# Five of the 36 input loads issued as two transfers, of 100 and of 28 partitions

## The chip, the cores and the metric

The kernel runs on one core of a Trainium2 chip. The metric is the device time of one execution in microseconds; the time of a kernel is the median of its runs. A separate execution of each kernel was recorded by the hardware profiler, and everything called "the profile" or "the trace" below comes from that one execution. The engines are named as the profile names them: PE (TensorE matmul), PEld (TensorE weight load), DVE (VectorE), ACT (ScalarE), POOL (GpSimd) and SP (SyncE, which here does nothing but issue DMAs). "SPq" is SP's instruction queue. The DMA transfers run on 16 DMA engines.

## The reference

Two stages are computed in one kernel. The first is a retention recurrence over 768 steps for 4 batches and 8 heads of 64 dimensions, the second a token mixer whose weights come from its own input:

```python
def _attn_ref(q, k, v):                       # q, k, v: (4, 8, 768, 64) float32
    gamma = 1.0 - 2.0 ** (-5.0 - np.arange(H, dtype=np.float32))
    scale = 1.0 / np.sqrt(D)
    for t in range(S):
        state = gamma[None, :, None, None] * state + np.einsum('bhd,bhe->bhde', k[:, :, t], v[:, :, t])
        y[:, :, t] = scale * np.einsum('bhd,bhde->bhe', q[:, :, t], state)
    return y

def _moe_ref(x, w_q, w_k, w_out):             # x: y as (4, 768, 512)
    wq, wk = x @ w_q, x @ w_k
    W_tok = scale * np.einsum('bsd,btd->bst', wq, wk)
    mixed = np.einsum('bst,btd->bsd', W_tok, x)
    return np.maximum(mixed, 0.0) @ w_out
```

The output is (4, 768, 512) in float32.

## The kernel before

**Tiling.** The 768 steps of a batch are three *pairs* of two 128-token chunks; four batches make the pairs 0 to 11. For each pair three loads bring q, k and v: 256 tokens of all 8 heads, 512 KB each. Partition g of a load holds the tokens 2g and 2g+1 of the pair, so each of the 128 partitions gets, for each of the 8 heads, one contiguous run of 2 x 64 floats, 512 bytes. That makes 128 x 8 = 1,024 runs of 512 bytes in a load.

**Loads.** `LOADS` (line 53) is the order of the loads, written out by hand: `... q3 w v3 k4 q4 k5 v4 q5 o1 o0 v5 k6 q6 v6 q7 k7 v7 k8 q8 v8 q9 k9 k10 v9 q10 k11 v10 q11 v11`, then the stores `s0 s5 ...`. `w` is the two small projection weights, `o0` and `o1` are four transfers of `w_out`. All of them are issued by SP, in this order (one half of k0 alone is issued by ACT). `load_pair` (line 157) issues the transfer of a pair: one `dma_start` over 128 partitions. The staging tiles `q_st`, `k_st`, `v_st` are 7 slots of three pairs each; a slot is loaded anew once the three pairs in it have been cast.

**Casts.** Before TensorE can use a load, another engine casts it to bf16: `cq`, `ck` and `cv` (`cv` also multiplies by a power of the decay, `fv`). `ORDER` (line 16) is one list of all steps, written out by hand; the letter behind a step is the engine that takes it (A for ACT, V for DVE, P for POOL). Every engine executes its own steps strictly in this order, so a step that waits holds back all later steps of its engine. `ck.5.0:P` is the cast of the first chunk of k of pair 5, on POOL. For the pairs from 2 on a `ck` or a `cv` of one chunk is two instructions of 64 partitions; the copies stand in the profile under the helper's lines 133 (ACT) and 134 (POOL, DVE), the `cv` under line 619.

**The steps that read the five loads of the change**, with their engines:

| load | steps | what stands behind them on the engine |
|---|---|---|
| v3 | `cv.3.0:P`, `cv.3.1:P` | `cq.4:P`, `ck.5.0:P`, `cv.4.0:P` |
| v4 | `cv.4.0:P`, `cv.4.1:P` | `WO.1:P` (a cast of `w_out`), `cv.5.0:P`, `cv.5.1:P`, `cq.6:P` |
| k7 | `ck.7.0:P`, `ck.7.1:P` | `ck.8.0:P`, `ck.8.1:P` |
| q9 | `cq.9:A` | `es.7.1:A`, `ck.9.1:A` |
| q10 | `cq.10:P` | `cv.9.1:P`, `cv.10.0:P` |

**The rest of a pair.** TensorE transposes k and q (`trk`, `trq`, lines 648 to 685), forms the scores `sc` (707), the running state `st` (758), the parts of y (`in` 744, `ia` 778), transposes x (`xt` 811, 818), projects it (`wqk` 841, 850), accumulates `zm` over a batch (875), and for each pair computes `mx` (894) and the output projection `pj` (916). DVE and ACT evict what TensorE leaves in PSUM. The last steps are `pj` and the evictions `eo`, after which SP issues the last stores (line 945).

Of the kernel before, what the change touches and what calls it, by code (L numbers as in the profile page):

```python
# [59 lines left out]
OBUFS = 9  # L60
CASTS = dict(k=6, v=6, q=4)
WBYTES = 1024
OBYTES = 2048
KQS = 2

# [2 lines left out]
def kernel(  # L68
# [15 lines left out]
    nc = tc.nc  # L84
# [4 lines left out]
    C = 128  # L89
    G = C // 2  # L90
    NP = S // (2 * C)
    NG = B * NP
    NDM = DM // 128
    HP = H // 2
# [48 lines left out]
    def slot(key):  # L143
        if key not in slots:
            slots[key] = stage_pool.tile([128, 3 * 2 * H * D], FP32, name=key + "_st", tag="st")
        return slots[key]
# [8 lines left out]
    SOURCES = {"k": k, "q": q, "v": v}  # L155

    def load_pair(name, p, half=None, eng=None):
        st = pairs[p]
        st[name + "_st"] = slot(name + str(p // NP)).rearrange(
            "p (cp x hp j d) -> p cp x hp j d", cp=NP, x=2, hp=HP, j=2  # L160
        )[:, p % NP]
        xs = slice(0, 2) if half is None else slice(half, half + 1)
        (eng or nc.sync).dma_start(
            out=st[name + "_st"][:, xs].rearrange("g x hp j d -> g (x hp) (j d)"),
            in_=SOURCES[name][
                p // NP, xs.start * HP : xs.stop * HP, p % NP * 2 * C : (p % NP + 1) * 2 * C, :
            ].rearrange(
                "h (g j) d -> g h (j d)", j=2
            ),
        )  # L170

    def load_batch(name, b):
        st = slot(name + str(b))
# [19 lines left out]
    def load_weights(token):  # L193
# [5 lines left out]
        else:  # L199
# [3 lines left out]
            for i in range(2):  # L203
                a = 2 * n + i
                nc.sync.dma_start(
                    out=st[:, i], in_=moe_w_out[128 * a : 128 * a + 128, :], max_dma_last_dim=WBYTES
                )
        wstages[token] = st

    def load_token(token):  # L210
        if token[0] in "wo":
            load_weights(token)
        elif token[0] in "KQV":
            load_batch(token[0].lower(), int(token[1:]))
        else:
            load_pair(token[0], int(token[1:]))
# [3 lines left out]
    freed = {}  # L220

    load_pair("k", 0, 0, nc.scalar)
    load_pair("k", 0, 1, nc.sync)

    def more_loads():
        while queue:
            token = queue[0]
            if token[0] == "s":
                if not stored(token[1:]):
                    return  # L230
                queue.pop(0)
                continue
            key = slot_of(token)
            if key not in staged:
                n = len(staged)
                if n >= SLOTS and freed.get(staged[n - SLOTS], 0) < 3:
                    return
                staged.append(key)
            load_token(queue.pop(0))
# [64 lines left out]
    for cp in range(NP):  # L304
        nc.gpsimd.tensor_copy(
            out=fy1.rearrange("p (cp x) c hp -> p cp x c hp", x=2)[:, cp].rearrange("p x c hp -> p c x hp"),
            in_=fy[:, 2 * cp : 2 * cp + 2].rearrange("p c (hp x) -> p c x hp", x=2),
# [627 lines left out]
    def stored(name):  # L935
        p, _, j = name.partition("/")
        p, js = int(p), [int(j)] if j else [0, 1]
        if not all((p, i) in evicted for i in js):
            return False
        b, cp = divmod(p, NP)  # L940
        dst = out[b, cp * 2 * C : (cp + 1) * 2 * C, :].rearrange("(g j) m -> g j m", j=2)
        src = pairs[p]["o"]
        if j:
            dst, src = dst[:, int(j)], src[:, int(j)]
        nc.sync.dma_start(out=dst, in_=src, max_dma_last_dim=OBYTES)
        return True

    steps2 = dict(
# [6 lines left out]
        st=state1, es=es1, ia=ia1, **{"in": inter1}, ex=ex1,  # L955
# [48 lines left out]
```

## Time and profile before

| what | us |
|---|---|
| median of 3 runs | 98.84 (98.34 to 99.11) |
| the profiled execution, its own time | 97.45 |
| its span, first to last instruction | 95.7 |
| PE busy | 83.9 (88% of the span) |
| DVE busy | 73.4 (77%) |
| ACT busy | 67.3 (70%) |
| POOL busy | 65.2 (68%) |

The profiled execution took 97.45 us by the same clock as the runs, 1.75 us more than its span, and 1.39 us less than their median. The granted TensorE clock was 0.997 over the span. The page that the profiler leaves has busy times, a strip of 40 slices, the DMA queues, a chain of waits that is followed back from the last instruction, and the costliest groups of instructions. Here the strip shows POOL busy until slice 32 and then idle, and PE busy from slice 2 to the end. From HBM 20.19 MB were read and 6.29 MB written.

In the lines of the profile `v_st<-in_v_dram` is a load of v, `vs<-v_st,fv` its cast, and a bracket behind a timeline line is the idle time ahead of it with what ended it. A busy share over the whole span mixes stages with different limits; the waits of a stage tell more.

### The profile page before, as it was taken

To read this page: it belongs to the slowest core of one execution; us is meant where nothing else is said; L and a number is where in the kernel's file an instruction comes from. 1 tells how busy PE (TensorE), PEld (TensorE's weight loads), DVE (VectorE), ACT (ScalarE), POOL (GpSimd) and SP (SyncE) were. 2 spreads that over 40 slices of the span, in tenths; PEclk is the share of its full clock that TensorE was granted. 3 is DMA by queue.
4 is the path that set the end of the run, shared out by engine and by line. 5 is a ranking of instruction groups with operands and counts; after the bars stand their busy time and mean duration, and the time that the engine had idled before them with its cause. 6 is when DMAs were issued, how large, how long until landed. Compare 5 with 4: busy or idle time off the path is not lost.

```text
span 95.7 us, 3878 instructions
## 1 busy us (share of the span) xinstructions
PE 83.9 (88%) x1677; PEld 53.6 (56%) x1695; DVE 73.4 (77%) x105; ACT 67.3 (70%) x102; POOL 65.2 (68%) x85
## 2 busy tenths in 40 slices
PE   4999799695788989999998999999999999999920
PEld 1334565574666657546786558677675775644400
DVE  3243986979799996995999999998999966547400
ACT  4200439968775689799997999999999755455640
POOL 4696870798899795999999999899999920000000
PEclk9999999999999999999999999999999999999998
DMA  1999999999999999999999999999679000919992
GB/s 32 283 347 347 346 345 310 288 260 265 280 327 299 344 332 334 311 334 339 298 297 337 323 332 303 265 302 326 217 280 374 28 0 39 394 71 403 399 377 80
DMA packets 42929, 26.73 MB, mean 279 GB/s; under 512 B 1952, under 2 KB 39840, under 8 KB 42912
## 3 DMA queue, kind: packets, MB, share of 16 engines
q1 hardware_dynamic: 42384, 26.22, 87.9%
q10 hardware_dynamic: 528, 0.26, 0.9%
q8 instruction: 13, 0.21, 0.8%
q14 instruction: 4, 0.03, 0.1%
HBM read 20.19 MB, written 6.29 MB: 277 GB/s over the span
## 4 chain that ended last, share of the span: by engine, by line
PE 62%; DVE 10%; ACT 8%; POOL 8%; issue 7%; DVEq 0%; ACTq 0%
PE banks L916 17%; PE banks L381 10%; POOL ks L134 5%; DVE at_sb L719 4%; PE banks L778 4%; PE banks L894 3%; PE banks L707 3%; ACT ks L133 3%; POOL vs L619 3%; PE banks L850 3%; PE banks L818 3%; PE banks L758 3%; PE banks L841 2%; PE banks L875 2%; PE banks L648 2%
## 5 line engine op out<-in xcount | busy, mean ns | idle before, releaser
L619 POOL TENSOR_TENSOR vs<-v_st,fv 64x512 bf16<-64x512 f32 x36 | 37.6, 1043 | 4.5 <-DMA v_st<-in_v_dram 2.5
L719 DVE TENSOR_TENSOR at_sb<-banks,cmaskr 128x1024 bf16<-128x1024 f32 x20 | 23.8, 1215 | 0.7 <-PE banks L707 0.6
L916 PE MATMUL banks<-wout_sb,relu 128*128 128x512 bf16 x82 | 22.2, 380 | 1.1 <-issue 0.5
L133 ACT CAST ks<-k_st 64x512 bf16<-64x512 f32 (+1 forms) x25 | 15.8, 634 | 9.3 <-DMA k_st<-in_k_dram 8.8
L133 ACT COPY o_st<-banks 128x512 f32<-128x512 f32 x19 | 11.2, 588 | 3.6 <-PE banks L916 3.6
L792 DVE TENSOR_TENSOR x_nat<-banks,fy 128x1024 bf16<-128x1024 f32 x10 | 12.2, 1222 | 1.8 <-PE banks L744 1.5
L916 PEld LDWEIGHTS <-relu 128*128 128x128 bf16 x96 | 8.2, 98 | 9.0 <-issue 1.2
L909 ACT ACTIVATE relu<-banks 128x1024 bf16<-128x1024 f32 x11 | 11.3, 1024 | 1.6 <-PE banks L916 1.0
L381 PE MATMUL banks<-warm 128*128 128x512 bf16 x31 | 10.6, 479 | 1.8 <-DVE warm L255 1.3
L134 POOL CAST ks<-k_st 64x512 bf16<-64x512 f32 x16 | 11.1, 695 | 1.1 <-DMA k_st<-in_k_dram 0.2
L134 DVE COPY kq<-banks 128x1024 bf16<-128x1024 bf16 x14 | 9.4, 687 | 3.2 <-PE banks L431 1.9
L133 ACT COPY kq<-banks 128x1024 bf16<-128x1024 bf16 x10 | 10.0, 1012 | 2.5 <-PE banks L431 1.7
L134 POOL CAST qs<-q_st 128x1024 bf16<-128x1024 f32 (+1 forms) x7 | 6.9, 986 | 3.1 <-DMA q_st<-in_q_dram 2.7
L707 PE MATMUL banks<-kq 64*128 64x128 bf16 x160 | 7.5, 217 | 0.3 <-DVE xT L134 0.3
L778 PE MATMUL banks<-vs,at_sb 128*128 128x64 bf16 x160 | 7.3, 193 | 0.2 <-DVE at_sb L719 0.2
L850 PE MATMUL banks<-xT,wqk_w 128*128 128x256 bf16 x48 | 7.2, 273 | 0.0
L381 PEld LDWEIGHTS <-warm 128*128 128x128 bf16 x35 | 3.4, 115 | 5.8 <-issue 3.4
L778 PEld LDWEIGHTS <-at_sb 128*128 128x128 bf16 x160 | 5.9, 98 | 1.1 <-DVE at_sb L719 0.3
L707 PEld LDWEIGHTS <-kq 64*128 64x128 bf16 x160 | 4.8, 94 | 3.0 <-issue 2.8
L133 ACT COPY xT<-banks 128x1024 bf16<-128x1024 bf16 x5 | 5.1, 1013 | 1.7 <-PE banks L818 1.6
L134 DVE COPY xT<-banks 128x1024 bf16<-128x1024 bf16 x7 | 4.8, 688 | 1.7 <-PE banks L818 0.8
L133 ACT CAST qs<-q_st 128x1024 bf16<-128x1024 f32 x5 | 5.2, 1049 | 1.1 <-DMA q_st<-in_q_dram 1.0
(83 smaller groups left out, 130.4 us busy)
## 6 DMA issues: line engine op xcount, KB each, us to landing
q_st<-in_q_dram SPq DMA_DIRECT2D x12, 512.0 KB, 6.6
v_st<-in_v_dram SPq DMA_DIRECT2D x12, 512.0 KB, 6.3
k_st<-in_k_dram SPq DMA_DIRECT2D x11, 512.0 KB, 7.1
out_dram<-o_st SPq DMA_DIRECT2D x9, 512.0 KB, 3.6
out_dram<-o_st SPq DMA_DIRECT2D x6, 256.0 KB, 2.3
w_st<-in_moe_w_out_dram SPq DMA_DIRECT2D x4, 256.0 KB, 5.2
k_st<-in_k_dram ACTq DMA_DIRECT2D x1, 256.0 KB, 3.8
k_st<-in_k_dram SPq DMA_DIRECT2D x1, 256.0 KB, 3.5
```

What stands on the lines that cost most here:

```text
L133: return nc.scalar.copy(out=out, in_=in_)
L134: return ENGINES[e].tensor_copy(out=out, in_=in_)
L381: nc.tensor.matmul(out=bank32(b), lhsT=warm[:, 0:128], rhs=warm, start=True, stop=True)
L619: ENGINES[e].tensor_tensor(out=tokens_st(p, "v")[rows(j), c].rearrange("p hp x d -> p (hp x) d"), in0=pair_st(p, "v")[rows(c), :, j], in1= ...
L707: nc.tensor.matmul(out=ps[:, x, hi, c, :], lhsT=st["kT"][rows(x), hp, c, :], rhs=st["qT"][rows(x), hp, c, :], start=(hi == 0 and c == 0), ...
L719: ENGINES[e].tensor_tensor(out=st["at", half].rearrange("p x hi c t -> p (x hi c) t"), in0=st["at_ps", half].rearrange("p (n t) -> p n t", ...
L758: nc.tensor.matmul(out=state_ps[rows(x), hp, :], lhsT=st["ks"][:, c, hp, x, :], rhs=st["vs"][:, c, hp, x, :], start=(cp == 0 and c == 0 an ...
L778: nc.tensor.matmul(out=y[:, x, c, hp, :], lhsT=st["at", half][:, x, hi, c, :], rhs=st["vs"][:, c, hp, x, :], start=first1(p, x), stop=Fals ...
L792: nc.vector.tensor_tensor(out=st["x"].rearrange("p c a i n -> p (c a i n)").rearrange("p (m x d) -> p x m d", x=2, d=D), in0=st["y_ps"].re ...
L850: nc.tensor.matmul(out=st["w_ps"][:, 128:384], lhsT=wqk_sb[:, a, DH:], rhs=st["xT"][:, a].rearrange("p c t -> p (c t)"), start=False, stop ...
L909: nc.scalar.activation(out=dst, in_=st["mx_ps"], func=ACT.Relu)
L916: nc.tensor.matmul(out=bank32(b), lhsT=st["relu"][:, a, j, :], rhs=wout_sb[:, a, :], start=(a == 0), stop=(a == NDM - 1),)
```

## The change

`load_pair` looks up the load's name in a table of cut points. Five loads are in it, each cut at partition 100; each of these is issued as two `dma_start`s one after the other on the same queue, partitions 0 to 99 and 100 to 127. All other loads have one piece, as before. The stores get the same loop with an empty table, so they stay one transfer.

```diff
 WBYTES = 1024
+PARTS = {'v3': (100,), 'v4': (100,), 'k7': (100,), 'q9': (100,), 'q10': (100,)}
+SPLIT = {}
 OBYTES = 2048
...
-        (eng or nc.sync).dma_start(
-            out=st[name + "_st"][:, xs].rearrange("g x hp j d -> g (x hp) (j d)"),
-            in_=SOURCES[name][
-                p // NP, xs.start * HP : xs.stop * HP, p % NP * 2 * C : (p % NP + 1) * 2 * C, :
-            ].rearrange(
-                "h (g j) d -> g h (j d)", j=2
-            ),
-        )
+        dst = st[name + "_st"][:, xs].rearrange("g x hp j d -> g (x hp) (j d)")
+        src = SOURCES[name][
+            p // NP, xs.start * HP : xs.stop * HP, p % NP * 2 * C : (p % NP + 1) * 2 * C, :
+        ].rearrange("h (g j) d -> g h (j d)", j=2)
+        cuts = [0, *PARTS.get(name + str(p), ()), C]
+        for lo, hi in zip(cuts, cuts[1:]):
+            (eng or nc.sync).dma_start(out=dst[lo:hi], in_=src[lo:hi])
...
-        nc.sync.dma_start(out=dst, in_=src, max_dma_last_dim=OBYTES)
+        cuts = [0, *SPLIT.get(name, ()), G * 2]
+        for lo, hi in zip(cuts, cuts[1:]):
+            nc.sync.dma_start(out=dst[lo:hi], in_=src[lo:hi], max_dma_last_dim=OBYTES)
```

## The prediction

> **What bounds the kernel now.** I read the page first, then the instruction queue of SP in order of time, then the idle gaps of POOL, then the chain of waits where POOL hands over to PE.
>
> ```profile
> PE 83.9 (88%) x1677; PEld 53.6 (56%) x1695; DVE 73.4 (77%) x105; ACT 67.3 (70%) x102; POOL 65.2 (68%) x85
> ...
> DMA  1999999999999999999999999999679000919992
> ...
> q8 instruction: 13, 0.21, 0.8%
> ```
>
> PE is the busiest engine. The DMA engines are busy without a break until slice 28 (67 us), so the loads are a stream that can set the pace too. The third line is traffic that the kernel did not issue: 13 packets of 16 KB that carry instructions. They use the same DMA engines.
>
> SP's queue, in order of time (start, duration):
>
> ```profile
> 1.28 0.50 SPq L163 DMA_DIRECT2D q_st<-in_q_dram  x1
> 1.82 0.57 SPq L163 DMA_DIRECT2D v_st<-in_v_dram  x1
> ...
> 10.67 1.40 SPq L163 DMA_DIRECT2D v_st<-in_v_dram  x1
> 12.12 3.02 SPq L163 DMA_DIRECT2D k_st<-in_k_dram  x1
> ...
> 22.68 2.43 SPq L163 DMA_DIRECT2D k_st<-in_k_dram  x1
> ...
> 42.60 2.52 SPq L163 DMA_DIRECT2D k_st<-in_k_dram  x1
> ...
> 55.85 2.82 SPq L163 DMA_DIRECT2D k_st<-in_k_dram  x1
> ```
>
> An issue that nothing holds up takes 0.5 us. Later ones take 1.4, which is the pace at which the DMA engines drain: SP waits for room. Four take 2.4 to 3.0. Instruction packets of 0.95 us start at 13.29, 23.67, 42.26 and 56.21 us, inside three of these four issues and 0.34 ahead of the other. (The rest of the packets go with shorter stops, such as 1.80 at 48.12; the longest issue of all, 3.32 at 33.24, follows four short ones for `w_out` that had filled the queue.) So one held-up DMA engine stops SP, and with it the supply of all sixteen.
>
> The trace also has sixteen landing marks for each transfer, one per DMA engine. Before 13 us a transfer's marks lie within 0.45 us and each comes exactly 1.512 us after the same mark of the transfer ahead: every engine moves 64 runs and one closing mark, 65 packets of 23.3 ns, eight rows each. It is a limit of each engine by packets, not of a shared pipe: the 256 KB transfers of `w_out`, with runs of 1 KB, land 0.68 us apart (385 GB/s against 347). For q2, behind the packet of 13.29, fifteen marks lie at 14.76 to 15.24 as expected and the sixteenth at 16.46. The others are unmoved, so the packet hit one engine, the one that had been twelfth to land.
>
> Where the loads reach the computation, POOL's timeline:
>
> ```profile
> 24.29 4.37 POOL L619 TENSOR_TENSOR vs<-v_st,fv 64x512 bf16<-64x512 f32 x4 [0.54 <-DMA v_st<-in_v_dram]
> ...
> 31.69 4.36 POOL L619 TENSOR_TENSOR vs<-v_st,fv 64x512 bf16<-64x512 f32 x4 [0.51 <-DMA v_st<-in_v_dram]
> ...
> 38.10 4.38 POOL L619 TENSOR_TENSOR vs<-v_st,fv 64x512 bf16<-64x512 f32 x4 [0.94 <-DMA v_st<-in_v_dram]
> ```
>
> These are the casts of v3, v4 and v5; the brackets are idle time ended by their loads. After 38.10 POOL has no gap until 77, so when v5 lands sets POOL's schedule from there on. It reaches PE twice:
>
> ```profile
> 50.33 0.97 POOL ks L134
> 51.30 0.05 issue
> 51.35 0.37 PE banks L648 x13
> ...
> 63.97 1.05 POOL vs L619
> 65.02 0.04 issue
> 65.06 0.32 PE banks L758 x8
> ```
>
> PE's matmuls start 0.32 us late at 51.35 and 0.39 late at 65.06 (spacing of starts, less the usual spacing of the line). Elsewhere from 36 to 92 us PE hardly pauses. So a gain in loads is worth at most about 0.7 us, while a loss at v5 goes through whole.
>
> **The change part by part.** *Shares.* A 128-row load gives each engine 8 rows. No transfer of another height is in the trace. If the shares stay equal, as all marks show for 128, 100 rows go to ten engines with 10 each (10 is the largest divisor of 100 up to 16) and 28 rows to fourteen with 2 each. If both start from the same first engine, ten engines get 12 rows (96 runs, 2 marks: 98 x 23.3 ns = 2.28 us, +0.77), four get 2 rows (0.40 us, -1.12) and two get none (-1.51). The other bound is an even spread, 0. I take the first, since every transfer of the trace is shared equally. The Trainium skill, "DMA: Bandwidth & Descriptors", section "Why a DMA increments its semaphore by 16 and not by 1", states this rule, with the lowest-numbered engines used; no run before shows it.
>
> *SP.* Five more issues at 0.5 us. The split issues stand among ones that last 1.3 to 1.8 us because SP waits for room, which covers them; without cover each costs 0.5.
>
> *Waits.* Each cast of the five loads now waits for both pieces. Behind v3 and v4 on POOL stand all later casts; k7, q9, q10 have slack: k7 lands 46.61 and is cast at 47.98, q9 54.30 and 56.96, q10 61.68 and 65.07. A delay below 1.4 us there costs nothing.
>
> *The stream, if the engine with the instruction packets is among the six light ones.* v3: the ten heavy engines now land at 23.11 to 23.59, plus 0.77 is 23.9 to 24.4; the late engine's 24.22 goes. The cast starts at 24.4, 0.1 later. Then k4, q4, k5 at 1.51 each and v4 at 2.28: 24.4 + 4.5 + 2.3 = 31.2 against 31.62; the packets of 23.67 and 28.40 fall on an engine that has time to spare. POOL is free at 31.3, so v4's cast starts 0.4 earlier. q5, four `w_out` pieces (0.68 each) and v5: 31.2 + 5.7 = 36.9 against 38.03. POOL is then free at 37.16 - 0.4 = 36.8, so v5's cast starts at 37.0 instead of 38.10, 1.1 earlier. Of that PE can take 0.32 at 51.35 and 0.39 at 65.06. I take 0.5 of the 0.7, because DVE and ACT are 89 to 99% busy around those two places (47 to 52 and 60 to 65 us) and can only follow in part. Nothing is late next but PE itself. Span 95.7 - 0.5 = 95.2, profiled 97.45 - 0.5 = 96.95, median 98.84 - 0.5 = 98.3.
>
> **Rivals.** *The instruction engine is a heavy one.* Then the same engine that lands last gets 0.77 more each time: v3 24.22 to 25.0, v4 31.62 to 33.15, v5 38.03 to 39.6. POOL has no gap behind it, and PE waits already at 51.35 and 65.06, so the end moves by the whole 1.5: 100.3, slower. ACT's cast of q5 would slip from 33.73 to 34.7, within the 1.5. The later three add nothing (q10: 61.68 + 3.8 = 65.5, cast at 66.6). It decides as soon as two splits together cost more than the 0.5 to 1.1 us of spread by which the late engine trails the rest. Blind odds are ten in sixteen; that the engine was twelfth to land speaks against, if landing follows the engines' numbers.
>
> *The relief is not used.* SP waits for the fullest engine, now one of ten, and the light ones run dry: v3 and v4 each cost 0.77, less the 1.1 by which the late engine trailed at v3 (24.22 against the first mark's 23.11): 1.54 - 1.1 = 0.4 at v5, so 98.84 + 0.4 = 99.2.
>
> *Even spread.* Nothing changes but five closing marks per engine, 0.1 us in all on the stream: 98.8. The skill's same page, section "Rules for kernel authors", speaks against the change: two transfers to disjoint partition halves "serialize", as both use all 16 engines; by it the result would be this one. The row of equal shares decides for me, as 100 is no multiple of 16.
>
> **How the numbers follow.** Chances: relief used 0.42 (98.3; 97.6 to 98.9), relief not used 0.15 (99.2; 98.8 to 99.9), even spread 0.10 (98.8), heavy engine 0.33 (100.3; 99.5 to 101). The likeliest gives 98.3. One per cent, 97.85 or 99.83, is about what a measurement here tells from no change. Faster by more: a third of the first case, 0.14. Slower by more: 0.30 of the last and 0.02 of the second, 0.32. The rest is 0.54. The range 97.6 to 100.6 leaves out the lowest tail of the first case and the highest of the last, about 0.15 in all. The first three cases alone would lie between 97.6 and 99.9.
>
> **What would show it.** Right: v3's cast about where it was, v5's cast near 37.0, SP's stops of 2.4 to 3.0 us shorter behind v4 and k7, and PE's late starts at 51.35 and 65.06 gone. Heavy engine: v5's cast near 39.6 with POOL's bracket near 2.4. Not used: v5's cast within 0.5 of 38.1. Wrong altogether: more than 0.77 per split, if ten engines writing other rows than before are slower per packet than 23.3 ns.

## The result and the profile after

The changed kernel takes 99.16 us (median of 20 runs, 98.04 to 101.81), the kernel before 98.29 (median of 20, 96.71 to 101.31). The ratio is 1.0133, with a 95% interval from 1.0085 to 1.0181: slower by about 1.3%, where 0.5% faster was forecast. (The ratio leaves out disturbed executions, which the medians contain, so it is not the quotient of the two.) The profiled execution took 99.38 us with a span of 97.7; that of before 97.45 and 95.7. So the two traces differ by 2.0 us of span, more than the runs do on the whole, and the amounts read from them below are those of this pair of executions.

The page after, busy time by engine and the strips of DMA share and throughput:

```profile
PE 83.8 (86%) x1677; PEld 53.7 (55%) x1695; DVE 73.2 (75%) x105; ACT 67.1 (69%) x102; POOL 65.4 (67%) x85
...
DMA  1999999999997999999999999999999400919992
GB/s 27 280 344 347 346 343 317 274 257 263 286 276 210 262 350 337 324 314 268 242 291 281 286 242 316 272 263 318 342 365 390 174 10 0 372 66 405 395 384 106
```

The throughput before, in the same slices:

```profile
GB/s 32 283 347 347 346 345 310 288 260 265 280 327 299 344 332 334 311 334 339 298 297 337 323 332 303 265 302 326 217 280 374 28 0 39 394 71 403 399 377 80
```

The engines have the same work as before. The strip of the DMA engines stands at 9 up to slice 31, but for a 7 in slice 13, where before it stood at 9 up to slice 28 and then fell to 6 and 7. Meanwhile the throughput falls: 210 and 242 GB/s in slices 13 and 20, against 299 and 298 before. The DMA engines seem occupied and move less.

SP's queue after, the issues around v3 and v4 (x2 is a split load):

```profile
18.09 1.41 SPq L199 DMA_DIRECT2D w_st<-in_moe_w_k_dram  x1
19.53 1.58 SPq L171 DMA_DIRECT2D v_st<-in_v_dram  x2
21.16 0.40 SPq L171 DMA_DIRECT2D k_st<-in_k_dram  x1
21.60 1.22 SPq L171 DMA_DIRECT2D q_st<-in_q_dram  x1
22.86 3.33 SPq L171 DMA_DIRECT2D k_st<-in_k_dram  x1
26.24 3.27 SPq L171 DMA_DIRECT2D v_st<-in_v_dram  x2
29.55 0.69 SPq L171 DMA_DIRECT2D q_st<-in_q_dram  x1
```

SP gets rid of both pieces of v3 in 1.58 us, about as long as the one transfer took before (1.51), then stops for 3.33 us in the issue of k5, which stopped it for 2.43 before. The issue of q5 begins at 29.55; before it began at 27.00:

```profile
27.00 1.44 SPq L163 DMA_DIRECT2D q_st<-in_q_dram  x1
```

POOL's timeline after, the casts of v3, k5, v4 and v5:

```profile
24.74 4.37 POOL L620 TENSOR_TENSOR vs<-v_st,fv 64x512 bf16<-64x512 f32 x4 [0.98 <-DMA v_st<-in_v_dram]
...
31.13 1.28 POOL L136 CAST ks<-k_st 64x512 bf16<-64x512 f32 x2 [0.85 <-DMA k_st<-in_k_dram]
33.64 4.36 POOL L620 TENSOR_TENSOR vs<-v_st,fv 64x512 bf16<-64x512 f32 x4 [1.23 <-DMA v_st<-in_v_dram]
...
39.97 4.38 POOL L620 TENSOR_TENSOR vs<-v_st,fv 64x512 bf16<-64x512 f32 x4 [0.87 <-DMA v_st<-in_v_dram]
```

v3's cast starts 0.45 later than before (24.29), v4's 1.95 later (31.69) and v5's 1.87 later (38.10). The forecast for v5 was 37.0.

The chain of waits after, from 26 to 38 us (start, duration, what):

```profile
26.24 1.40 SPq L171
27.64 0.04 issue
27.69 1.82 SPq L171
29.51 0.04 issue
29.55 5.74 DMA q_st<-in_q_dram
35.30 0.02 issue
...
36.32 0.37 ACT z_sb L135
36.70 0.05 issue
36.74 0.39 PE banks L895 x4
```

Here is where most of the time goes. In this stretch the chain no longer runs through the engines: it goes back along SP's queue, through both pieces of v4 and the load of q5, which lands at 35.30 instead of 33.14. ACT waits for it (before, on the third line, it did not):

```profile
35.37 1.04 ACT L135 CAST qs<-q_st 128x1024 bf16<-128x1024 f32 x1 [0.95 <-DMA q_st<-in_q_dram]
36.32 0.36 ACT L135 CAST z_sb<-banks 128x256 bf16<-128x256 f32 x1
...
33.73 1.05 ACT L133 CAST qs<-q_st 128x1024 bf16<-128x1024 f32 x1
```

Behind the cast of q5 on ACT stands the eviction `ez.0` (`z_sb`), for which PE waits with the first output mixing (line 894 before, 895 after). That starts at 36.74, before at 35.10: 1.64 later. The wait for q5, 0.95, is not all of it. The other 0.7 came earlier, at k4, the load right behind the split v3. It lands at 27.59 instead of 26.88, and ACT waits 2.21 us for it instead of 1.11 (after, then before):

```profile
27.61 1.24 ACT L135 CAST ks<-k_st 64x512 bf16<-64x512 f32 x2 [2.21 <-DMA k_st<-in_k_dram]
...
26.90 1.25 ACT L133 CAST ks<-k_st 64x512 bf16<-64x512 f32 x2 [1.11 <-DMA k_st<-in_k_dram]
```

At the end of the program the last eviction starts 2.07 later (93.77 against 91.70). The rest is made at 51 to 57 us, where DVE waits for v7 (the last line is that cast before, without a wait):

```profile
49.16 1.21 DVE L720 TENSOR_TENSOR at_sb<-banks,cmaskr 128x1024 bf16<-128x1024 f32 x1
51.40 3.99 DVE L620 TENSOR_TENSOR vs<-v_st,fv 64x512 bf16<-64x512 f32 x4 [1.02 <-DMA v_st<-in_v_dram]
55.42 1.22 DVE L793 TENSOR_TENSOR x_nat<-banks,fy 128x1024 bf16<-128x1024 f32 x1
...
48.78 4.07 DVE L619 TENSOR_TENSOR vs<-v_st,fv 64x512 bf16<-64x512 f32 x4
```

v7 stands in the queue right behind the split k7 and lands at 51.30 instead of 48.17. PE then waits 0.9 us for `x_nat` at 56.7 and falls from 1.5 behind to 2.5, of which it regains 0.5 later. So in all three places the load that holds up the kernel is the one right behind a split load: k4, q5 and v7.

**What a split load costs.** A landing mark is what one DMA engine leaves when its part of a transfer is done. The trace has ten marks for each 100-row piece and fourteen for each 28-row piece, besides one mark that comes with the end of the issue. From the median mark of the transfer ahead to the median mark of the 100-row piece it is 2.74, 2.74, 2.75, 2.58 and 2.52 us for the five loads, and from there to the ten late marks of the 28-row piece 0.50 to 0.87 more. The ten engines thus need 3.1 to 3.6 us for a split load (median 3.35), where a whole one takes 1.51. The prediction had 2.28.

### The profile page after: what moved, and what is told of

It reads as the page before. It is cut to its first block, busy times and chain, and to the rows that moved or that the text cites. A ratio compares the mean times of both kernels' runs of the same rounds, so it can differ in the third digit from the quotient of the medians.

```text
span 97.7 us, 3885 instructions
## 1 busy us (share of the span) xinstructions
PE 83.8 (86%) x1677; PEld 53.7 (55%) x1695; DVE 73.2 (75%) x105; ACT 67.1 (69%) x102; POOL 65.4 (67%) x85
## 4 chain that ended last, share of the span: by engine, by line
PE 53%; SPq 29%; DMA 6%; ACT 3%; issue 3%; DVE 1%; DVEq 0%; ACTq 0%
SPq L171 26%; PE banks L917 20%; DMA q_st<-in_q_dram 6%; PE banks L779 4%; PE banks L708 4%; PE banks L851 4%; PE banks L895 3%; SPq L199 3%; PE banks L842 3%; PE banks L759 3%; PE banks L819 2%; PE banks L876 2%; PE banks L745 2%; PE banks L649 2%; PE banks L682 1%
```

## The experiments

The theories: **A**, ten engines carry 12 rows instead of 8, and this holds up the stream, at the usual 23.3 ns a packet. **B**, the packets themselves become slower, because a transfer that spans fewer partitions lets several DMA engines write over the same path at the same time (a *path* is the way by which a few groups of four partitions are written). **C**, two transfers for a load cost by themselves, by the second issue and the wait on both. All kernels below are the changed one with another table of cuts, except where a diff says more.

| run | cuts of the load | ratio to before, 95% interval |
|---|---|---|
| the change | 100, all five | 1.0133 (1.0085 to 1.0181) |
| e1_v3_v4 | 100, v3 and v4 | none |
| e2_k7_q9_q10 | 100, k7, q9, q10 | none |
| e8_v3_only | 100, v3 | 1.0061 (1.0004 to 1.0119) |
| e9_v4_only | 100, v4 | 1.0092 (1.0032 to 1.0151) |
| e3_by_heads | 4 and 4 heads, all five | 0.9988 (0.9926 to 1.005) |
| e4_cut_64 | 64, all five | 1.0117 (1.0027 to 1.0206) |
| e5_cut_32_96 | 32 and 96, all five | 1.0116 (1.0064 to 1.0168) |
| e6_cut_120 | 120, all five | 1.013 (1.0033 to 1.0227) |
| e7_cut_32_72 | 32 and 72, all five | none; one time, 97.67 |
| e10_cut_32_72_again | 32 and 72, all five | 1.0153 (1.0047 to 1.0259) |

### Which of the five loads count

```diff
-PARTS = {'v3': (100,), 'v4': (100,), 'k7': (100,), 'q9': (100,), 'q10': (100,)}
+PARTS = {'v3': (100,), 'v4': (100,)}                  # e1
+PARTS = {'k7': (100,), 'q9': (100,), 'q10': (100,)}   # e2
```

> Only v3 and v4 are cut at 100. In the trace of the changed kernel q5 lands 2.2 us later and TensorE starts the first output mixing of batch 0 (L895) about 1.6 us later; the rest of the loss (0.5 us) shows at 55 to 57 us, behind v7. Theory A (the ten engines with more rows hold up the stream; what is ahead of 38 us counts): about +1.5 us, 1.5% slower than before, the whole of the change or nearly. Theory C (a load in two transfers costs by itself, in issue time and waits): 2/5 of the change, +0.5%.

> Only k7, q9 and q10 are cut at 100. Theory A: these loads land 1 to 3 us ahead of their use, but v7 stands right behind k7 and has only 0.6 us to spare in the profile of before; the stream behind k7 is 1.6 to 2 us later less the trail of the late engine (about 1.2), so DVE waits some 0.2 to 0.5 us for v7: between no change and +0.5%. Theory C: 3/5 of the change, +0.8%.

With v3 and v4 alone the median is 100.24 (98.48 to 101.0, 6 runs) against 98.34 (96.96 to 101.95, 17 runs); with the other three 98.69 (96.64 to 99.74, 6 runs). Neither has an interval, and six runs that lie 2.5 and 3.1 us apart settle neither cost, nor which of the two is larger. The traces show the places. With v3 and v4 alone q5 lands at 34.84, ACT waits for it, and the first output mixing starts at 36.29 instead of 35.10; about 0.4 of that 1.2 us is there already at 25 us. The last eviction is 1.16 late (92.86 against 91.70), and DVE does not wait for v7:

```profile
34.91 1.05 ACT L135 CAST qs<-q_st 128x1024 bf16<-128x1024 f32 x1 [0.84 <-DMA q_st<-in_q_dram]
```

With the other three DVE waits 0.41 us for v7, as expected; what that costs at the end is not shown. Each early load alone:

> Only v3 is cut at 100. The ten engines with 12 rows need some 3.2 us for it (81 packets at about 33 ns, 17 at about 40) against 1.51, 1.7 more; the engine that fetches instructions trailed by about 1.1 there and has 2 rows now. So the stream behind v3 is 0.6 to 1.2 us later, v4 lands 0.6 to 1.0 later, q5 0.6 to 1.0 later, of which ACT's cast of q5 has 0.6 to spare: between +0.0 and +0.5 us, 0 to 0.5%.

> Only v4 is cut at 100. q5 stands right behind it and has nowhere to catch up: v4's second piece and q5 land 0.6 to 1.2 us later, ACT's cast of q5 starts up to 0.6 us later, POOL's cast of v4 0.6 to 1.0 us later, v5 0.6 to 1.0: +0.3 to +0.8 us, 0.3 to 0.8%. If v3 and v4 add up, the two alone give the loss of the run with both (+1 to 1.9%).

By the ratios both are slower, by 0.6% and 0.9%, above the upper ends of what was expected (0.5% and 0.8%), with intervals that reach back into it; the sum, 1.5%, agrees with the loss of the whole change within its interval. But the plain medians don't show it (98.36 and 98.72 against 98.68 for the kernel before), so what one early load costs alone is not settled. Their single traces can't be used for the place of the loss: in both, PE is already 1.6 us behind the trace of before at the wait on `x_nat` (30.8 us against 29.2), and about as far behind at 36.7. In both, the granted clock was 0.77 to 0.81 from 16 to 24 us, where it was 1.00 before, and with v4 alone PE fell behind there, ahead of the split load.

### Two transfers, same rows

```diff
-        cuts = [0, *PARTS.get(name + str(p), ()), C]
+        cuts = [0, *PARTS.get(name + str(p), ()), dst.shape[1]]   # cut at 4 of 8 heads
         for lo, hi in zip(cuts, cuts[1:]):
-            (eng or nc.sync).dma_start(out=dst[lo:hi], in_=src[lo:hi])
+            (eng or nc.sync).dma_start(out=dst[:, lo:hi], in_=src[:, lo:hi])
```

> The same five loads are two transfers each, but of 4 heads by 128 partitions: every engine has its 8 rows in both, the issues and the waits on two transfers stay. Theory A and theory B: as before, within 0.3%, with all sixteen landing marks in step. Theory C: as the change, +1.3%.

No difference: 0.9988, and the interval's upper end of 1.005 excludes the 1.3% of theory C. The second piece of four heads comes 0.81 us behind the first (median of the five, two of which took 1.05 and 1.08; 33 packets at 23.3 ns are 0.77). Throughput while split loads ran (k7, then q10), and on the last line for whole loads before. The columns are stretch, length, the busy times of PE, PEld, DVE, ACT and POOL, the clock, the DMA share and GB/s. The DMA share is the time that packets took, over sixteen engines, so it can pass 1 where an engine's packets overlap:

```profile
44.65:46.45 1.80, 1.48 (x52) 1.13 (x51) 0.80 (x2) 1.27 (x3) 1.78 (x2) 1.00 1.08 324
...
60.30:61.80 1.50, 1.50 (x46) 1.31 (x42) 1.50 (x3) 1.44 (x4) 1.44 (x2) 1.00 1.06 319
...
43.30:44.80 1.50, 1.40 (x57) 1.16 (x54) 0.69 (x1) 1.48 (x3) 1.43 (x3) 1.00 1.13 334
```

That is nearly the pace of a whole load (q9, not shown, had 305). In the changed kernel the 100-row piece of k7 and then its 28-row piece went at

```profile
45.00:47.80 2.80, 2.65 (x74) 1.80 (x70) 1.93 (x3) 2.59 (x4) 2.65 (x4) 1.00 1.02 248
47.80:48.30 0.50, 0.50 (x28) 0.46 (x24) 0.50 (x1) 0.50 (x2) 0.50 (x1) 1.00 1.19 176
```

### Equal shares, fewer rows

`PARTS` cuts all five at 64: each piece gives each of sixteen engines 4 rows.

> The same five loads cut at partition 64: 64 rows are 4 for each of sixteen engines, twice, so all engines carry the same. Theory A (shares alone, at 23.3 ns a packet): as before, within 0.3%. Theory B (the packets themselves are slower when a transfer spans fewer than 128 partitions, because several engines then write the same group of partitions; in the changed kernel the 100-row pieces went at about 33 ns a packet and the 28-row pieces at about 41): the 64-row pieces take 35 to 45 ns a packet, 2.3 to 2.9 us for a load against 1.51, and the time is 1 to 2% longer than before.

Slower by 1.2% (0.3 to 2.1), though no engine carries more than before: theory A can't say why. The second pieces (partitions 64 to 127) of k7, q9 and q10:

```profile
45.40:46.50 1.10, 1.05 (x26) 0.63 (x18) 0.76 (x2) 1.08 (x2) 1.02 (x2) 1.00 1.25 231
...
54.30:55.60 1.30, 1.30 (x38) 0.80 (x33) 1.30 (x2) 1.12 (x3) 1.18 (x3) 1.00 1.14 217
...
61.40:62.50 1.10, 1.05 (x18) 0.48 (x19) 1.10 (x2) 1.10 (x2) 0.98 (x3) 1.00 1.15 209
```

The DMA share stands at 1.14 to 1.25 while only 209 to 231 GB/s are moved: sixteen engines are occupied, and each packet takes longer. A second piece comes 1.11 us behind the first (median of five), 34 ns a packet, and the first piece 1.47 us behind the load ahead of it, so a load cut at 64 takes 2.58 us, as theory B expected. The records of single packets say the same: in the second pieces of k7 and q10 the median 512-byte packet took 42 ns, before (43.3 to 44.8 us) and with the cut by heads 27 ns.

### The same 64 rows, in another place

Cuts at 32 and 96, so that the middle piece has 64 rows too, 4 for each of sixteen engines, but the partitions 32 to 95.

> The same five loads in three transfers: partitions 0 to 31, 32 to 95 and 96 to 127. All are shared equally by sixteen engines (2, 4 and 2 rows each), so no engine carries more than before. The middle piece has 64 rows like the pieces of the run cut at 64, but lies across the middle. Theory B in the form of shared write paths (groups of 4 partitions, with the groups 32 apart on one path and those of the two halves of 64 apart): the middle piece reaches all sixteen paths with one engine on each, so its marks come 33 packets of 23.3 ns behind those of the piece ahead (0.77 us), while the third piece, 17 packets on eight paths, takes 0.6 to 0.7 us instead of 0.40. Theory B in the form 'a transfer of few rows is slow' (on the memory side, or by its size): the middle piece is as slow as in the run cut at 64, 1.0 to 1.3 us. Time: 0 to 1.2% above before.

The middle piece and behind it the third, of q9 and of q10:

```profile
56.30:57.10 0.80, 0.26 (x4) 0.00 (x0) 0.80 (x2) 0.62 (x2) 0.68 (x3) 1.00 1.17 284
57.10:57.80 0.70, 0.66 (x18) 0.49 (x19) 0.70 (x1) 0.58 (x1) 0.70 (x1) 1.00 1.19 233
62.90:63.80 0.90, 0.90 (x15) 0.45 (x10) 0.90 (x2) 0.90 (x3) 0.80 (x2) 1.00 1.04 306
63.80:64.40 0.60, 0.60 (x13) 0.18 (x13) 0.60 (x2) 0.60 (x2) 0.58 (x1) 1.00 0.68 172
```

284 and 306 GB/s for the middle, 233 and 172 for the third (the DMA share of 0.68 says that engines stood idle in the last of them); k7, not shown, has 307 and 256. In the middle pieces of these three the median packet took 27 ns, as in a whole load. By the marks the middle piece comes 0.93 us behind the first (1.12, 1.39, 0.88, 0.82, 0.93) and the third 0.69 behind the middle (0.40 at the full pace). So equal shares and equal size are fast or slow by the partitions that they cover, which is what theory B in the form of shared write paths says, and rules out the form in which a transfer of few rows is slow. One rival is left: the rows that are read from HBM move with the partitions, so the runs don't separate the write side from the read side. It isn't the full pace (0.77): the middle piece runs behind a slow one, whose marks lie 1.2 us apart or more. As the two outer pieces are slow, the kernel is slower by 1.2% all the same.

The Trainium skill, "SBUF — State Buffer", section "Door 1: The DMA port swizzle (why `[64,N]` ≈ `[32,N]`)", states the rule: partitions that differ by 32 share one of sixteen ports, those that differ by 64 don't, so that 0 to 63 reach only eight; its measured figure for them is 196 GB/s at 1 MiB. The traces agree: 209 to 231 GB/s for 64 to 127 (203 for a load cut at 64 as a whole, 512 KB in 2.58 us) and 284 to 307 for 32 to 95, which by this rule reach all sixteen.

### Eight rows for an engine, in a run

> The same five loads cut at 120: fifteen engines with 8 rows each, then eight engines with 1 row. Theory A (shares at 23.3 ns): eight engines get 0.2 us more, the rest nothing, no change in time. Theory B: the 120-row piece is slow, because eight rows in a run cross two groups of partitions and two engines meet in each; 30 to 40 ns a packet, 2 to 2.5 us for a load, and +0.7 to 1.5%. As to the engine that fetches instructions: if it is one of the engines 10 to 13, as one late mark among the light engines of k7's second piece in the changed kernel says, then a late mark shows in 120-row pieces behind a fetch and never in the 8-row pieces.

Slower by 1.3%. The 120-row piece, at 8 rows for each of fifteen engines, takes 2.74 us (median; 42 ns a packet, 30 to 40 were expected) where the 128-row load at 8 rows for each of sixteen takes 1.51, so the smaller transfer is the slower:

```profile
44.50:47.30 2.80, 2.51 (x69) 1.72 (x68) 1.62 (x3) 2.75 (x4) 2.65 (x4) 1.00 1.18 255
```

Where the instruction engine is: in v4's 120-row piece one mark comes at 33.92, the others until 32.59, and the eight marks of the 8-row piece lie at 32.17 to 32.66, so there the late engine isn't among the lowest eight. In the changed kernel q7's last mark is at 47.32, and k7's 28-row piece has a mark at 47.72, 0.40 later, the time of 17 packets, ahead of all heavy engines (48.5 on). So it was among the light four there. But in q10, cut at 120, the 8-row piece has one mark at 66.54 and the others until 65.40, a late mark that was not expected. No record names the engine, so where it is stays open.

### Ten engines, no shared path

Cuts at 32 and 72: the middle piece is on ten engines, 4 rows each, by theory B one engine on each path.

> The same five loads in three transfers: 0 to 31 (sixteen engines, 2 rows), 32 to 71 (ten engines, 4 rows) and 72 to 127 (fourteen engines, 4 rows). The middle piece has an uneven share, ten engines of sixteen, but by theory B one engine on each write path: its ten marks come 0.77 us behind the piece ahead, as if it were a part of a whole load. If a transfer on ten engines is slow in itself, they come 1.0 us or more behind. The third piece has two engines on six of its ten paths and should take 0.9 to 1.3 us.

The middle piece comes 0.74, 0.92, 0.65, 0.83 and 0.99 us behind the first, median 0.83, so ten engines aren't slow in themselves. The third piece, with two engines on six of its paths (by the rule these are eight, not ten), takes 1.42 us (43 ns a packet), above the expected 0.9 to 1.3. The one time was 97.67, below the median of 98.78 before, so the kernel was run again with an interval:

> The kernel of e7_cut_32_72, now with an interval; its one profiled time was 97.67. By the write paths its pieces of 32 and 56 rows are slow (34 and 43 ns a packet), but ten engines carry only 10 rows, the late engine at most 6, and the casts of the first 64 rows need not wait for the last piece (v4's cast started 0.7 us earlier than before in that profile). If that weighs as much as the slow pieces, it is as before or up to 0.5% faster; if slow pieces decide, +0.5 to +1%.

1.0153 (1.0047 to 1.0259): slower, by more than expected (by the plain medians, 99.44 against 98.68, 0.8%), and the single time is put down to scatter. The paces came again (middle 0.77, third 1.27, medians). No kernel of this study is shown to beat the one before.

The pace by piece, as the median step between marks over the five loads:

| piece | engines | us | ns a packet |
|---|---|---|---|
| 128 rows, undisturbed | 16 | 1.51 | 23.3 |
| 128 rows, 4 heads | 16 | 0.81 | 25 |
| 40 rows, 32 to 71 | 10 | 0.83 | 25 |
| 64 rows, 32 to 95 | 16 | 0.93 | 28 |
| 64 rows, 64 to 127 | 16 | 1.11 | 34 |
| 100 rows, 0 to 99 | 10 | 2.74 | 34 |
| 32 rows, 0 to 31 | 16 | 0.62 | 36 |
| 32 rows, 96 to 127 | 16 | 0.69 | 41 |
| 120 rows, 0 to 119 | 15 | 2.74 | 42 |
| 56 rows, 72 to 127 | 14 | 1.42 | 43 |
| 64 rows, 0 to 63 | 16 | 1.47 | 45 |

The four rows on top are the pieces that, by theory B, give each engine a path of its own. Why the others lie between 34 and 45 ns, and the two halves of a load cut at 64 so far apart, isn't explained by these runs.

## Why the prediction was wrong

**The term that failed is the price of a split load**, "98 x 23.3 ns = 2.28 us, +0.77". The count of packets was right, the 23.3 ns were not: this is the pace of a transfer over all 128 partitions. The 100-row piece went at 34 ns and the 28-row piece at 30 to 50, so a split load cost 3.35 us, +1.84. Of the 1.84, the uneven shares at full pace are the 0.77 of the prediction; the other 1.07 is the slower packets. That slow packets alone make the kernel slow is shown by the cut at 64, that the second transfer does not by the cut by heads, and that the partitions matter by the cuts at 32 and 96; that it is the write paths is argued from the rule. The prediction named this under what would make it "wrong altogether" and gave it no price and no chance. So v5's cast came at 39.97 and not at 37.0, and SP's stop in the issue of k5 grew from 2.43 to 3.33 us where it should have shrunk. With the measured price the prediction's own sum for two split loads, less the 1.1 us by which the late engine trailed, gives 2.6 us of delay at v5 (an estimate); 1.87 was measured.

**The number.** The 99.16 us lie inside the stated range and are almost the 99.2 of the rival "the relief is not used". That is luck. The range starts from 98.84, a median of three runs; twenty runs put the kernel before at 98.29. And the sign of that rival, v5's cast within 0.5 of 38.1, did not appear.

**Shares**: right. The marks show ten engines and fourteen. But uneven shares aren't needed to make the kernel slow: the cut at 64 has even ones and loses 1.2%.

**The light engine**: open; k7 and v4 above speak for it, q10 with the cut at 120 does not. If it was light, that brought nothing: the ten others were 1.84 us later for each split, more than the 1.1 us by which the late engine had trailed. The rival with a heavy instruction engine had the direction right and its end time (+1.5 us) near the measured 1.3%. Of its signs v5's cast came (39.97, expected near 39.6), POOL's bracket did not (0.87, expected near 2.4), and its price per split, 0.77, was the same wrong one.

**SP's issues**: right, no cost shows (the cut by heads, 0.9926 to 1.005).

**Waits**: partly wrong. "Each cast of the five loads now waits for both pieces" doesn't hold: v3's first cast step reads partitions 0 to 63 and started at 24.74, behind the first piece (24.67) and ahead of the second (26.45).

**The path to the end**: the prediction followed v5 to POOL and took a slip of ACT's cast of q5 for a part of the same loss. v5 did slip by 1.87, but the chain went through k4 and q5 to ACT and PE at 36.74. For the late loads it held that k7, q9 and q10 have slack, which they do, and overlooked v7 behind k7, with 0.6 us of slack, where PE lost 1.0 us in this profile and regained half of it later.

**The gain at PE** (0.32 and 0.39 us) came in part, for another reason: no load came earlier, but PE itself came later to the places where POOL hands over, and regained 0.1 us at the first and 0.3 at the second.

## What to carry to other kernels

In this kernel a load's pace depended on which partitions it covered, and not only on how evenly its rows were shared: before cutting a transfer by partitions, ask which DMA engines will then write over the same path at the same time. If a load has to be cut, cut it along the free dimension, for which no cost showed here. Look for the damage at the load right behind the cut one. And price a transfer of a new shape from both sides, with a slower pace as one of the cases, when every row of the trace comes from one shape.

## What the runs showed of the hardware

One 16 KB instruction packet occupied one DMA engine for about 0.95 us: in the trace of before, one of q2's sixteen marks came 1.2 us behind the rest. Next to four of these packets an SP issue took 2.4 to 3.0 us instead of 1.4; that SP waits for the fullest engine is inferred from that. A transfer on fewer than sixteen engines gave one mark at the end of its issue, ahead of all data, besides one for each engine (eleven for ten, fifteen for fourteen). And the DMA share of the profile doesn't tell a stream that runs well from one that is held up: it was 1.13 at 334 GB/s before and 1.25 at 231 GB/s with the cut at 64.
